# A gated mix of a long convolution and a mixer on one core: products as pairs of 128x64 tiles, and a new order of all tasks

## The chip, the cores and the metric

The kernel runs on one core of one Trainium2 chip. The metric is the device time of one execution in microseconds (us), the median of several runs; lower is better. A core has TensorE (PE: matrix products; its weight loads are listed apart as PEld), VectorE (DVE), ScalarE (ACT), GpSimd (POOL) and SyncE (SP), which here issues nearly all DMAs.

## The reference

`x` (2048 x 640, the input `q`) goes through two branches, and a gate mixes them.

```python
x = A_q
g = _sigmoid((x * gate_w).sum(-1, keepdims=True))
a = _A_ref(x, A_k, A_v, A_shift_k, A_ssm_k, A_ssm_D)
b = _B_ref(x, B_w1, B_w2, B_w3, B_w4)
return g * a + (1 - g) * b
```

Branch A: `k` is shifted and summed with four taps per channel and multiplied by `v` (that is `kv`); `kv` is convolved along the 2048 rows with a filter of 2048 taps per channel (the reference does it by an FFT of length 4096), `kv * ssm_D` is added, and the result is multiplied by `q`. Branch B, the mixer: layernorm, product with w1 (640x640), gelu, four groups of channels shifted by +1, -1, +2, -2 rows, product with w2, residual (`x1`); then layernorm, w3 (640x1536), gelu, w4 (1536x640), residual.

## The kernel before, in words

The whole kernel is a list of 778 **tasks**. Each has an engine (some have a choice), a duration that its author wrote down, what it reads and writes, and the buffers that it takes from pools and gives back. The text `ORDER` at the head of the file is a permutation of the task numbers; a letter behind a number names the engine where there is a choice. The function `place` walks the order, keeps a clock for each engine with the written durations, and picks buffers by it; then the tasks are issued in just this order. So the order of the text fixes the order on each engine. `place` also decides how many filler matmuls (L256, products of zeros that nobody reads) stand ahead of a PE task in the first microseconds, once the task `fill` has passed.

The convolution is a Fourier transform in steps, all of them matrix products on PE:

- `trh.0` to `trh.4` (L851) transpose the filter, loaded as `SK`; `evt.*` (L388 on ACT, L390 on DVE) copy the result to `HT`, and `dfold` (L857, POOL) adds the `ssm_D` row to it.
- `s1h.*` (L903) is the first step for the filter; it reads `HT` (the first four `evt` copies at least) and the matrix `BM`, which the DMA pair `bm` (L504) builds from the sine table. `s1x.*` (L905) is the same for `kv`. Their results are copied (`e1h`, `e1x`) to `FS` and written to memory (`wFh`, `wFx`, L935).
- `s2h`, `s2x` (L957) read them back (`rF`, L949) in ten parts; `pa`, `pb` (L972, DVE) multiply the spectra; `s3` (L985) goes back, `wG` writes.
- `s4.0` to `s4.15` (L1023) is the last step, one 128-row block each: two products of 512 columns and two of 128, each with a 128x64 weight tile, so that two run side by side in the two halves of the array. DVE then does `yq` (L1029, times the gate and q) and `ad` (L1056), or for the rows 12 to 15 `ax` (L1037) and `fo` (L1043), which add the mixer's part.

`kv` is made on DVE in four groups `kv3` to `kv0` of eight operations of 128x2560 each (L870, L874, L878): taps, sums and the product with `v`. The taps are the row `CJ`: `cjp` (POOL, L390) turns the order of 2560 numbers, `wCJ` (L516) writes them, `rCJ` (L518) reads them back on all partitions.

The mixer: `st1` (mean and variance of a block, DVE L578 to L582 or ACT L586, L587), `rs1` (POOL L595 to L598, the power -1/2), `nm1` (L602 or L632), `tr1` (L610, PE transposes, two blocks each), `ev1`, `evh` (copies to `xnT`), `w1.G.part` (L690, or L694 for part 4), `g1` (ACT L707, gelu), `w2.s` (L716), `x1.s` (DVE L723, residual), `sq.s` (ACT L728). The second half has `ve2`, `st2` (POOL), `nm2`, `dt2` (L805, a transposing DMA), `w3.c.fb` (L813, five products of 128x512), `g2` (ACT L820), `w4.s` (L827; L834 for the rows 12 to 15, as two tasks `.0` and `.1`): twelve products of 512 columns and twelve of 128. `t2.s` (DVE L842) adds it to x.

Each PE task has a **mode**, the shape of its weight tiles: `f` is 128x128, `c32` and `c64` are 128x32 and 128x64, `r64` 64x128, `q32` 64x32, `s32` 32x64. `place` adds 0.096 us where the mode of a PE task differs from that of the one before. In the kernel before, only `s4` has `c64`; `w3` and `w4` are all `f`.

PSUM is one pool of eight banks ("U"). A task takes one bank or an aligned pair, and the copy that reads it gives it back. At most eight DMAs of SP were under way at a time in the trace.

Of the kernel before, what the change touches and what calls it, by code (L numbers as in the profile page):

```python
# [37 lines left out]
41 0 23 5 29 94v 6 7 9 3 19 11 17 4 25 1 2 31 32 15 18 8 10 63v 12 13 14 26 27 87v 61a 85a 64 62 95v 104v 65v 28  # L38
42 88 86 393 24 44 96 209 43 210 55a 66v 89v 67 395 56 68a 58a 53v 54 97v 34 90a 30 399 396v 400v 57v 91 397 40
394a 93a 98 59 99v 100v 92v 60v 101 103v 143 147 16 20p 33 149 398a 102a 77a 145 79v 21 45 150 80 391 71v 72 46  # L40
22 144 148 69v 392v 82v 74a 121 39 122 450 70 78 146 107a 73v 458 35 75 451v 401p 438 37 81v 76v 439a 151 83
113v 123 36 459a 38 456 152 457a 49 84v 108 114 454 452 115v 116 125 455a 453a 110v 129 117v 446 444 126 460
118v 403 404 405 124 127 447a 162 163 406 130 128 156 157 440 105a 441a 407 159 153 154 106 160 461 47 445a 402
131 158 109a 155 442 111 132 137 443a 112a 408 161 462 466 48 138 409 463a 448 134 135 468 215p 216 449 164 140
469a 467a 119 413 141 51 221p 165 470 410 50 411 120a 166 222 223v 464 465a 167 474 471a 173 475a 174 171 217a
480 168 476 187 191 481a 482 193 477a 172 473 192 188 412 414 218 483a 478 169 195 189 170 181 415 416 417 479a
472 418 419 421 422 182 178 179 485 196 194 190 486 423 488 219a 484 225a 489a 175 220 487a 492 176 493a 136 203
424 204 494 425 490 206 498 207 495a 200 201 491a 420 426 427 428 430 502 499a 226 177 504 224 505a 211 503a 506
500 227 496 501a 239 507a 133 497 228 240 508 142 429 184 185 139 247 431 432 433 434 435 436 248 233 510 512
# [12 lines left out]
692v 691a 693 345 302 341 298 299 723 725 346 342 300 696 728 359 371 705 707 729 710 714 360 372 361 365 362
# [22 lines left out]
class Plan:  # L85
# [13 lines left out]
    def add(self, name, eng, dur, fn, r=(), w=(), use=(), acq=(), rel=(), roles=(), after=(), mode=None, nbytes=0):  # L99
# [3 lines left out]
        t.kept = None  # L103
        t.acq = [(a, 1, a == "U") if isinstance(a, str) else a for a in acq]
# [43 lines left out]
    def place(self, order):  # L148
# [6 lines left out]
        mode, bw, flying, self.kept = None, 0.0, [], None  # L155
        start, end = [None] * n, [None] * n
        for i in order:
# [34 lines left out]
            else:  # L192
                d = t.dur
# [17 lines left out]
                free[e] = end[i] = at + d  # L211
            for (o, p, k) in t.rel:
# [143 lines left out]
def build(env, nc, io):  # L356
# [55 lines left out]
    add("ident", "POOL", 0.55, c_id, r=["iotb"], w=["ID"])  # L412
# [100 lines left out]
    add("cjp", {"POOL": 3.2, "ACT": 2.3}, 0, lambda t: copy(t, env["VC"][0:1, 3, :, :],  # L513
# [106 lines left out]
    for s0 in pairs:  # L620
        nm = []
        for s in (s0, s0 + 1):
            st1[s] = add(f"st1.{s}", {"DVE": 1.26, "ACT": 1.73}, 0, lambda t, s=s: f_st1(t, s), r=[("x", s, 0), ("x", s, 1)],
                         w=[("MV", s)])
            add(f"rs1.{s}", "POOL", 0.85, lambda t, s=s: f_rs1(t, s), r=[("MV", s), "c0"], w=[("RS", s)])
        for s in (s0, s0 + 1):
# [7 lines left out]
            nm1[s] = add(f"nm1.{s}", {"DVE": 0.445, "ACT": 1.2}, 0, f_nm1, r=[("RS", s), ("x", s, 0), ("x", s, 1)],  # L634
# [154 lines left out]

    LATE, late = (12, 13, 14, 15), {}  # L790
    for c in range(4):
        nT, nP = None, f"x1nT{c % 2}"
        for s0 in (4 * c, 4 * c + 2):
            ss = (s0, s0 + 1)
            add(f"ve2.{s0}", {"DVE": 0.42, "POOL": 1.5}, 0, lambda t, s0=s0: f_ve2(t, s0), r=[("x", s, 0) for s in ss] + [("S2", s) for s in ss],
                w=[("v2", s0)])
            add(f"st2.{s0}", "POOL", 1.5, lambda t, s0=s0: f_st2(t, s0), r=[("v2", s0)] + [("x", s, 0) for s in ss],
# [12 lines left out]
        for fb in range(12):  # L810
            def w3(t, fb=fb, nP=nP):
                for kb in range(5):
                    nc.tensor.matmul(env.PS[:, t.buf["U"][0], :], lhsT=env["W3"][:, kb, 128 * fb:128 * fb + 128],  # L813
                                     rhs=env.nT(int(nP[-1]))[:, :, kb, :], start=(kb == 0), stop=(kb == 4))
            t = add(f"w3.{c}.{fb}", "PE", 1.09, w3, r=["W3"] + [("x1nT", 4 * c + i) for i in range(4)], rel=[(nT, nP)],
                    use=[h2] if h2 else [], acq=[ONE] if h2 else [ONE, "h2"], after=("xnT",), mode="f")
# [5 lines left out]
        for s in range(4 * c, 4 * c + 4):  # L822
            def w4(t, s=s, o=h2):
                m = env.Uf(t.buf["U"][0])
                for (c0, c1) in ((0, 512), (512, 640)):
                    for fb in range(12):
                        nc.tensor.matmul(m[:, c0:c1], lhsT=env["h2T"][:, o.buf["h2"][0], fb, 128 * (s % 4):128 * (s % 4) + 128],  # L827
                                         rhs=env["W4"][:, fb, c0:c1], start=(fb == 0), stop=(fb == 11))
# [270 lines left out]
```

## Time and profile before

| | us |
|---|---|
| median of 3 runs (lowest, highest) | 226.26 (226.03, 226.96) |
| span of the profiled execution, first to last instruction | 225.3 |
| what the median has beyond that span | 1.0 |
| PE busy | 214.4 (95%) |
| DVE busy | 188.8 (84%) |
| ACT busy | 154.7 (69%) |
| POOL busy | 45.9 (20%) |
| moved by DMA | 57.90 MB, mean 257 GB/s |

The profile is of one execution. For that execution there is its span alone, not a device time of its own; the median of the runs is 1.0 us above the span. A row of a timeline reads: start, length, engine, line, operation, output <- input with partitions x elements, count, and in brackets how long the engine was idle before and who ended it. A row of the chain reads: start, length, what, count. A matmul's own length covers its way through the array: 379 ns for 512 columns, though a stretch of 25 of them takes 5.50 us of the chain, 220 ns each; so a small gap between two matmuls does not show as idle PE, and PE's busy share says little of switches between tile shapes.

### The profile page before, as it was taken

The numbers are of one execution on the slowest core, as the hardware profiler recorded it, in microseconds if no ns is written. First come the engines' busy times: TensorE is split into PE (matmuls) and PEld (weight loads), VectorE is DVE, ScalarE is ACT, GpSimd is POOL, SyncE is SP. The second block draws the span as 40 slices with busy tenths as digits, with TensorE's granted clock in tenths as the row PEclk, the third lists the DMA queues.
The fourth block names the chain that finished last, engine by engine and source line by source line (L and its number), as shares of the span: only waits on it lengthen the run. The fifth ranks groups of instructions, "written<-read, shape, count | busy, mean of one in ns | idle before, by whom it ended". The sixth has DMA issues, their size and how long they took to land.

```text
span 225.3 us, 5017 instructions
## 1 busy us (share of the span) xinstructions
PE 214.4 (95%) x1978; PEld 104.2 (46%) x1998; DVE 188.8 (84%) x281; ACT 154.7 (69%) x225; POOL 45.9 (20%) x86
## 2 busy tenths in 40 slices
PE   3999999999999999999999999999999999999993
PEld 1576454556444444345543333334445554544462
DVE  7898897999999999997479989899767327988993
ACT  6988999699988999789568988878875002125000
POOL 7373451446100009920800000000000000000000
PEclk9999999999999999999999999999999999999998
DMA  6999998999999969979999969999982596888524
GB/s 194 274 335 244 238 245 255 292 225 355 322 210 368 205 231 298 378 254 246 237 390 311 305 190 288 279 323 340 221 269 87 160 414 188 256 268 249 166 58 116
DMA packets 39501, 57.90 MB, mean 257 GB/s; under 512 B 15027, under 2 KB 30645, under 8 KB 39478
## 3 DMA queue, kind: packets, MB, share of 16 engines
q1 hardware_dynamic: 39158, 57.27, 88.9%
q10 hardware_dynamic: 320, 0.33, 0.5%
q8 instruction: 15, 0.25, 0.4%
q14 instruction: 8, 0.07, 0.1%
HBM read 35.56 MB, written 18.36 MB: 239 GB/s over the span
## 4 chain that ended last, share of the span: by engine, by line
PE 72%; DVE 11%; DMA 9%; ACT 4%; issue 2%; POOL 1%; DVEq 0%; POOLq 0%
PE PS L813 18%; PE PS L827 17%; PE PS L716 9%; DMA C<-TRIG 7%; PE PS L834 6%; PE PS L957 5%; PE PS L690 4%; PE PS L985 4%; DVE VC L870 3%; DVE VC L874 3%; PE PS L1023 2%; DMA K<-in_A_k_dram 2%; ACT FS L388 2%; PE PS L256 2%; PE PS L903 2%
## 5 line engine op out<-in xcount | busy, mean ns | idle before, releaser
L820 ACT ACTIVATE h2T<-PS 128x512 bf16<-128x512 f32 x48 | 27.9, 605 | 28.4 <-PE PS L813 28.0
L827 PE MATMUL PS<-W,h2T 128*128 128x128 bf16 (+1 forms) x281 | 39.8, 297 | 0.4
L388 ACT CAST FS<-PS 128x1024 bf16<-128x1024 f32 x37 | 36.0, 1019 | 5.6 <-PE PS L905 3.5
L813 PEld LDWEIGHTS <-W 128*128 128x128 bf16 x240 | 21.1, 98 | 30.7 <-issue 9.4
L827 PEld LDWEIGHTS <-h2T 128*128 128x128 bf16 x288 | 22.2, 98 | 18.9 <-issue 1.9
L388 ACT CAST XH<-PS 128x1024 bf16<-128x1024 f32 x26 | 25.5, 1020 | 7.5 <-PE PS L957 7.4
L813 PE MATMUL PS<-x1nT,W 128*128 128x512 bf16 x120 | 28.5, 380 | 0.0
L813 PE MATMUL PS<-XB,W 128*128 128x512 bf16 x120 | 28.5, 380 | 0.0
L972 DVE TENSOR_TENSOR PP<-XH 128x2048 bf16<-128x2048 bf16 x20 | 23.7, 1220 | 3.1 <-ACT XH L388 2.8
L870 DVE TENSOR_TENSOR VC<-K,VC 128x2560 bf16<-128x2560 bf16 x16 | 23.7, 1491 | 1.7 <-DMA W<-in_B_w_dram 1.5
L716 PE MATMUL PS<-W,hsT 128*128 128x128 bf16 (+1 forms) x155 | 23.5, 297 | 1.0 <-ACT hsT L707 0.7
L842 DVE TENSOR_TENSOR x<-PS,x 128x640 bf16<-128x640 f32 x12 | 9.8, 824 | 13.7 <-PE PS L827 13.7
L690 PE MATMUL PS<-xnT,W 128*128 128x512 bf16 x80 | 19.2, 379 | 0.1
L716 PEld LDWEIGHTS <-hsT 128*128 128x128 bf16 x160 | 12.8, 98 | 13.1 <-DMA W<-in_B_w_dram 1.2
L874 DVE TENSOR_TENSOR VC<-VC 128x2560 bf16<-128x2560 bf16 x12 | 17.9, 1491 | 0.3
L390 DVE CAST XH<-PS 128x1024 bf16<-128x1024 f32 x14 | 16.9, 1220 | 1.2 <-PE PS L957 1.1
L1029 DVE SCALAR_TENSOR_TENSOR W<-PS,GG,QO 128x640 bf16<-128x640 f32 x16 | 13.6, 879 | 2.5 <-PE PS L1023 2.2
L388 ACT CAST GS<-PS 128x1024 bf16<-128x1024 f32 x12 | 12.0, 1016 | 3.9 <-PE PS L985 3.9
L256 PE MATMUL PS<-C 128*128 128x512 bf16 x34 | 10.7, 460 | 3.8 <-DVE C L507 3.7
L834 PE MATMUL PS<-W,h2T 128*128 128x128 bf16 (+1 forms) x94 | 13.3, 298 | 0.1
L723 DVE SCALAR_TENSOR_TENSOR x<-PS,x 128x640 bf16<-128x640 f32 x16 | 12.9, 820 | 0.3 <-PE PS L716 0.3
L957 PE MATMUL PS<-FX,TRIG 64*32 64x512 bf16 x320 | 12.4, 381 | 0.3 <-ACT GS L388 0.3
(115 smaller groups left out, 292.5 us busy)
## 6 DMA issues: line engine op xcount, KB each, us to landing
FH<-FS SPq DMA_DIRECT2D x8, 640.0 KB, 5.3
FXD<-FS SPq DMA_DIRECT2D x8, 640.0 KB, 5.4
FX<-FH SPq DMA_DIRECT2D x10, 512.0 KB, 5.8
FX<-FXD SPq DMA_DIRECT2D x10, 512.0 KB, 5.3
GX<-GD SPq DMA_DIRECT2D x8, 640.0 KB, 5.9
W<-in_B_w_dram SPq DMA_DIRECT2D x2, 1920.0 KB, 11.9
GD<-GS SPq DMA_DIRECT2D x8, 480.0 KB, 4.4
SK<-in_A_ssm_k_dram SPq DMA_DIRECT2D x5, 512.0 KB, 6.8
```

Source lines behind the costliest of these rows:

```text
L388: nc.scalar.copy(out=out, in_=in_)
L390: (nc.vector if t.on == "DVE" else nc.gpsimd).tensor_copy(out=out, in_=in_)
L690: nc.tensor.matmul(m[:, b, :], lhsT=W[:, 0, kb, 160 * fb:160 * fb + 128], rhs=rhs(kb, shifts[fb]), start=(kb == 0), stop=(kb == 4))
L716: nc.tensor.matmul(m[:, c0:c1], lhsT=env["hsT"][:, o.buf["hs"][0], fb, 128 * (s % 4):128 * (s % 4) + 128], rhs=env["W12"][:, 1, fb, c0:c1] ...
L813: nc.tensor.matmul(env.PS[:, t.buf["U"][0], :], lhsT=env["W3"][:, kb, 128 * fb:128 * fb + 128], rhs=env.nT(int(nP[-1]))[:, :, kb, :], star ...
L820: nc.scalar.activation(out=env["h2T"][:, o.buf["h2"][0], fb, :], in_=env.PS[:, t.buf["U"][0], :], func=ACT.Gelu_apprx_tanh)
L827: nc.tensor.matmul(m[:, c0:c1], lhsT=env["h2T"][:, o.buf["h2"][0], fb, 128 * (s % 4):128 * (s % 4) + 128], rhs=env["W4"][:, fb, c0:c1], st ...
L834: nc.tensor.matmul(env.PS[:, t.buf["U"][0], 0:c1 - c0], lhsT=env["h2T"][:, o.buf["h2"][0], fb, 128 * (s % 4):128 * (s % 4) + 128], rhs=env ...
L870: nc.vector.tensor_tensor(out=VC[:, o], in0=env["K"][:, a + 3 - j:a + 7 - j, :], in1=w, op=ALU.mult)
L874: nc.vector.tensor_tensor(out=VC[:, 1], in0=VC[:, 1], in1=VC[:, 2], op=ALU.add)
L957: nc.tensor.matmul(env.U(t.buf["U"][0])[32 * j:32 * j + 32, gp, :], lhsT=CRI()[64 * gp:64 * gp + 64, 32 * pc:32 * pc + 32], rhs=X[64 * gp: ...
L972: nc.vector.tensor_tensor(out=env["PP"][:, o.buf["PP"][0], a, :].rearrange("p (b c) -> p b c", b=2), in0=X.unsqueeze(1).broadcast_to([P, 2 ...
```

## The change

Three things are changed.

- **Tiles.** The function `halves_of` gives, for a task of mode `c64`, the two halves of 64 columns. With it, every product of `w3.3.*` (12 tasks), of `w4.8`, `w4.10`, `w4.11`, and of `w4.12` to `w4.15` is issued as two products with 128x64 weight tiles, side by side like those of `s4`, and these tasks have mode `c64`. That makes 228 products into 456 (144 of them had 512 columns, 84 had 128).
- **Durations in `place`.** Those of several GpSimd tasks (`ident`, `cjp`, `rs1`, `ve2`, `st2`, `dfold`) and of `st1` and `nm1` are other numbers, and DVE tasks of some kinds are not placed while `cjp` or `dfold` runs on GpSimd. This acts on the choice of buffers and on the count of fillers only.
- **Order.** `ORDER` is another permutation, with other engine letters.

```diff
 ORDER = """
-41 0 23 5 29 94v 6 7 9 3 19 11 17 4 25 1 2 31 32 15 18 8 10 63v 12 13 14 26 27 87v 61a 85a 64 62 95v 104v 65v 28
...
+23 5 6 0 7 1 9 3 11 12 104v 8 10 17 2 15 29 63v 64 94v 61a 32 25 28 97v 95a 55v 62 65v 66v 96 19 31 87v 67 98 53a 54 ...
...
+    LOCKS = ("nm1.", "nm2.", "kv", "pa.", "pb.", "pc.", "ad.", "ax.", "phase1", "phand", "phsmall")
...
+            t.lock, t.hold = t.name.startswith(self.LOCKS), t.name in ("cjp", "dfold")
...
+                if t.lock and e == "DVE" and held[0] <= at < held[1]:
+                    start[i] = at = held[1]
...
-    add("cjp", {"POOL": 3.2, "ACT": 2.3}, 0, lambda t: copy(t, env["VC"][0:1, 3, :, :],
+    add("cjp", {"POOL": 2.6, "ACT": 2.3}, 0, lambda t: copy(t, env["VC"][0:1, 3, :, :],
...
+    def halves_of(t):
+        return ((0, 64), (64, 64)) if t.mode == "c64" else ((0, P),)
+
     LATE, late = (12, 13, 14, 15), {}
+    COLS = (8, 10, 11, 12, 13, 14, 15)
...
-                    nc.tensor.matmul(env.PS[:, t.buf["U"][0], :], lhsT=env["W3"][:, kb, 128 * fb:128 * fb + 128],
-                                     rhs=env.nT(int(nP[-1]))[:, :, kb, :], start=(kb == 0), stop=(kb == 4))
+                    for q, w in halves_of(t):
+                        nc.tensor.matmul(env.PS[q:q + w, t.buf["U"][0], :], lhsT=env["W3"][:, kb, 128 * fb + q:128 * fb + q + w],
+                                         rhs=env.nT(int(nP[-1]))[:, :, kb, :], start=(kb == 0), stop=(kb == 4))
...
-                    use=[h2] if h2 else [], acq=[ONE] if h2 else [ONE, "h2"], after=("xnT",), mode="f")
+                    use=[h2] if h2 else [], acq=[ONE] if h2 else [ONE, "h2"], after=("xnT",), mode="c64" if c == 3 else "f")
...
-                        nc.tensor.matmul(m[:, c0:c1], lhsT=env["h2T"][:, o.buf["h2"][0], fb, 128 * (s % 4):128 * (s % 4) + 128],
-                                         rhs=env["W4"][:, fb, c0:c1], start=(fb == 0), stop=(fb == 11))
-            kw = dict(r=["W4"] + [("h2", c, fb) for fb in range(12)], rel=[(h2, "h2")], mode="f")
+                        for q, w in halves_of(t):
+                            a = 128 * (s % 4) + q
+                            nc.tensor.matmul(m[q:q + w, c0:c1], lhsT=env["h2T"][:, o.buf["h2"][0], fb, a:a + w],
+                                             rhs=env["W4"][:, fb, c0:c1], start=(fb == 0), stop=(fb == 11))
+            kw = dict(r=["W4"] + [("h2", c, fb) for fb in range(12)], rel=[(h2, "h2")], mode="c64" if s in COLS else "f")
```

The new order in the places that matter, by task names.

- SP, head, before: ldsk1 ldx4 ldCJ ldgw ldx0 ldx14 ldx2 ldsk2 ldD ldsk4 ldsk3 ldw1 ldx6 ldsk0 bm ldx10 wCJ ldk15 ldk11 rCJ. After: ldx4 ldx14 ldgw ldx2 ldCJ ldx0 ldx6 ldsk4 ldw1 ldx10 ldsk3 ldsk2 ldsk0 ldD ldsk1 wCJ bm ldk11 ldk15 rCJ. (`ldx` loads blocks of x, `ldsk` the filter, `ldk` k.)
- ACT, head, after: warm abs sin0 st1.4 st1.14 st1.2 st1.0 st1.8 sin1 sin st1.7 st1.9 ev1.14 g1.1.2 st1.6 g1.0.0 st1.11 g1.0.2 g1.0.4 g1.0.1 g1.0.3 nm1.6 evt.0 nm1.10 e1h.4. Before, six `st1` were on ACT and ten on DVE; after, nine and seven. evt.0 was on DVE and is on ACT.
- PE, head, after: tr1.4 tr1.14 tr1.2 tr1.0 fill gwm w1.1.2 w1.0.3 w1.0.0 w1.0.4 w1.0.2 trh.3 w1.0.1 trh.2 trh.0 tr1.8 trh.1 tr1.6 trh.4 s1h.4 s1h.5 w1.1.1 w1.1.3 s1h.6 w1.1.0 s1h.7 tr1.10. Before, `fill` came first, and 36 filler matmuls were issued; after, one.
- DVE, ahead of the kv groups, after: ... evt.4 st1.13 e1h.6 ev1.10 kv3.m2. From kv3 to kv0.v both orders hold 32 kv operations and 15 x1; before also nm2.2, after also sg.
- PE, last stage, before: w4.9 w4.6 | s4.6 s4.7 w3.3.0 w3.3.6 s4.2 s4.3 w3.3.1 ... , seven stretches of s4 among products of mode f. After: w4.7 w4.9 | w3.3.0 w3.3.4 w3.3.11 w3.3.10 s4.6 s4.7 w3.3.2 s4.3 s4.2 ... w4.12.1, all of one mode behind the bar; w4.10 and w4.11 stand behind the bar as well.
- Places where the mode of a PE task differs from the one before it: 97 before, 84 after. Of these, with c64: 14 before, 1 after; with q32 or s32 (the steps s2 and s3): 51 before, 57 after; with r64 or c32: 32 before, 26 after.

More of the change, by code (lines that the diff above doesn't have):

```diff
@@ L211, in place @@
                 free[e] = end[i] = at + d
+                if t.hold and e == "POOL":
+                    held = (at, end[i])
             for (o, p, k) in t.rel:
@@ L622, in build @@
         for s in (s0, s0 + 1):
-            st1[s] = add(f"st1.{s}", {"DVE": 1.26, "ACT": 1.73}, 0, lambda t, s=s: f_st1(t, s), r=[("x", s, 0), ("x", s, 1)],
+            st1[s] = add(f"st1.{s}", {"DVE": 1.37, "ACT": 1.7}, 0, lambda t, s=s: f_st1(t, s), r=[("x", s, 0), ("x", s, 1)],
                          w=[("MV", s)])
-            add(f"rs1.{s}", "POOL", 0.85, lambda t, s=s: f_rs1(t, s), r=[("MV", s), "c0"], w=[("RS", s)])
+            add(f"rs1.{s}", "POOL", 0.95, lambda t, s=s: f_rs1(t, s), r=[("MV", s), "c0"], w=[("RS", s)])
         for s in (s0, s0 + 1):
@@ L633, in f_nm1 @@
                                             scalar2=SS("RS")[:, c], op0=ALU.add, op1=ALU.mult)
-            nm1[s] = add(f"nm1.{s}", {"DVE": 0.445, "ACT": 1.2}, 0, f_nm1, r=[("RS", s), ("x", s, 0), ("x", s, 1)],
+            nm1[s] = add(f"nm1.{s}", {"DVE": 0.445, "ACT": 0.95}, 0, f_nm1, r=[("RS", s), ("x", s, 0), ("x", s, 1)],
                          acq=("xn",))
@@ L794, in build @@
             ss = (s0, s0 + 1)
[L795 removed]
+            add(f"ve2.{s0}", {"DVE": 0.42, "POOL": 4.0}, 0, lambda t, s0=s0: f_ve2(t, s0), r=[("x", s, 0) for s in ss] + [("S2", s) for s in ss],
                 w=[("v2", s0)])
[L797 removed]
+            add(f"st2.{s0}", "POOL", 3.5, lambda t, s0=s0: f_st2(t, s0), r=[("v2", s0)] + [("x", s, 0) for s in ss],
                 w=[("r2", s) for s in ss])
@@ L856, in build @@
         add(f"evt.{cb}", {"ACT": 1.86, "DVE": 1.23}, 0, evt, use=[t], rel=[(t, "U")], w=[("HT", cb)], after=("PRE",), roles=("HT",))
-    add("dfold", {"DVE": 0.5, "POOL": 0.9}, 0, lambda t: (nc.vector if t.on == "DVE" else nc.gpsimd).tensor_tensor(out=env["HT"][0:1, 0, :], in0=env["HT"][0:1, 0, :],
+    add("dfold", {"DVE": 0.5, "POOL": 1.5}, 0, lambda t: (nc.vector if t.on == "DVE" else nc.gpsimd).tensor_tensor(out=env["HT"][0:1, 0, :], in0=env["HT"][0:1, 0, :],
                                                                in1=env.early("DR", [1, D], BF16), op=ALU.add),
```

37 lines of the change are left out of this document (9 added, 28 removed), and 4 rows, old and new, of the table ORDER.

## The prediction

> **What bounds the kernel now.** I read the page's busy shares and chain first, then the windows of the stages, then the chain of the last stage.
>
> ```profile
> span 225.3 us, 5017 instructions
> PE 214.4 (95%) x1978; PEld 104.2 (46%) x1998; DVE 188.8 (84%) x281; ACT 154.7 (69%) x225; POOL 45.9 (20%) x86
> PE 72%; DVE 11%; DMA 9%; ACT 4%; issue 2%; POOL 1%; DVEq 0%; POOLq 0%
> ```
>
> PE is the bound on average. An average over stages says little, so the next view cuts the span at five events: first operation of the kv groups (37.33), end of the last one (96.97), first product of s2 (113.59), first product of s4 (186.30), end of PE (221.50).
>
> ```profile
> core 0: us, PE busy (x) PEld busy (x) DVE busy (x) ACT busy (x) POOL busy (x), PEclk, DMA share, GB/s
> 0.00:37.33 37.33, 32.35 (x277) 18.73 (x282) 31.53 (x96) 32.92 (x49) 18.99 (x44) 1.00 0.95 257
> 37.33:96.97 59.64, 58.65 (x421) 28.27 (x424) 58.31 (x64) 53.18 (x81) 21.84 (x27) 1.00 0.99 282
> 96.97:113.59 16.62, 16.34 (x123) 8.86 (x123) 10.58 (x26) 12.05 (x23) 5.10 (x16) 1.00 0.98 264
> 113.59:186.30 72.71, 72.02 (x927) 31.22 (x932) 56.40 (x55) 49.62 (x62) 0.00 (x0) 1.00 0.92 273
> 186.30:221.50 35.20, 35.04 (x242) 17.08 (x244) 31.51 (x41) 6.94 (x12) 0.00 (x0) 1.00 0.67 194
> 221.50:225.30 3.80, 0.02 (x1) 0.00 (x0) 0.41 (x2) 0.00 (x0) 0.00 (x0) 0.78 0.40 109
> ```
>
> The reader is to see that the stages have different limits. In the first, ACT (32.9 of 37.3) and DVE (31.5) are as full as PE, and part of PE's time is fillers:
>
> ```profile
> L256 PE MATMUL PS<-C 128*128 128x512 bf16 x34 | 10.7, 460 | 3.8 <-DVE C L507 3.7
> ```
>
> In the second, DVE is busy for 58.31 of 59.64 us: the kv groups are one chain on one engine, so what comes behind them (the last s1x, the write and read through memory, s2) moves with the **start of kv3**. From s2 on PE is busy 99% and decides; there the number of switches between tile shapes counts. What a switch costs is in the chain of the last stage.
>
> ```profile
> 186.34 0.66 PE PS L1023 x8
> 187.00 2.27 PE PS L813 x10
> 192.19 0.94 PE PS L1023 x12
> 199.59 5.50 PE PS L813 x25
> ```
>
> L813 is w3: 25 products take 5.50 and 10 take 2.27, so one costs (5.50-2.27)/15 = 0.215 us, and 2.27-10x0.215 = 0.12 is left over for the switch. L1023 is s4: four more products cost 0.94-0.66 = 0.28 us, and 0.66-0.56 = 0.10 is left. So **a switch costs 0.11 us** in either direction.
>
> **The change part by part. Tiles.** In the last stage 14 switches become 1: 13x0.11 = -1.43 us. In s2 and s3 the new order has 57 instead of 51: +0.66. The other six saved lie ahead of the end of kv, where DVE decides; they count nothing. Together **-0.77**.
>
> What the pairs themselves cost: an s4 block is one pair of 512 and one of 128 columns, 0.28 us. The same work with full tiles in w4 is 0.215 plus a 128-column product. Of these twelve in a row have to be loaded at their own pace:
>
> ```profile
> L834 PE MATMUL PS<-W,h2T 128*128 128x128 bf16 x48 | 3.2, 219 | 0.0
> L834 PEld LDWEIGHTS <-h2T 128*128 128x128 bf16 x96 | 7.3, 98 | 5.9 <-issue 0.5
> L1023 PEld LDWEIGHTS <-BT 128*64 128x64 bf16 x64 | 2.5, 109 | 3.6 <-issue 2.5
> ```
>
> In an unbroken stretch one of them costs about 0.06 us (the busy row's 3.2/48 = 0.067 still holds the tail of each dozen), so a pair of 512 and one of 128 should cost 0.275 with full tiles: the s4 block's 0.28 is the same within what can be read. The unknown is a dozen small pairs in a row, which s4 never has. Below: no loss, as in s4 (a gain is excluded: the columns streamed are as many). Above: the load of a half tile is 109-98 = 11 ns longer; if all of it shows, 84 pairs x 0.011 = +0.9. I take 0, because in s4 the loads behind a small pair had no more than that pair's 0.06 us either; both ends stay in the range.
>
> **Order, head.** Today kv3 waits for a DMA at its start, and the first product of s1h stands at 28.23:
>
> ```profile
> 28.23 0.38 PE L903 MATMUL PS<-HT,C 128*128 128x512 bf16 x1 [0.58 <-DVE HT L390]
> 37.33 1.49 DVE L870 TENSOR_TENSOR VC<-K,VC 128x2560 bf16<-128x2560 bf16 x1 [1.51 <-DMA W<-in_B_w_dram]
> ```
>
> The bytes that SP issues ahead of the taps (x, filter, w1, bm, eight blocks of k) are the same in both orders, so kv3 can hardly start ahead of 37.3. What the new order puts ahead of it is ACT: s1h.4 needs evt.0, and evt.0 now stands on ACT behind nine st1.
>
> ```profile
> 3.49 1.15 ACT L486 ACTIVATE PRE<-PRE,C 128x1024 f32<-128x1024 int32 x1 [1.28 <-DVE PRE L472]
> 4.67 2.56 ACT L484 ACTIVATE TRIG<-PRE,C 128x1024 bf16<-128x1024 f32 x3
> 7.14 0.72 ACT L586 ACTIVATE JK<-x 128x640 bf16<-128x640 bf16 x1
> 8.94 0.74 ACT L586 ACTIVATE JK<-x 128x640 bf16<-128x640 bf16 x1
> L388 ACT COPY xnT<-PS 128x1280 bf16<-128x1280 bf16 x4 | 4.9, 1227 | 1.9 <-DVE xnT L390 1.0 <-PE PS L610 0.9
> L707 ACT ACT_TABLE_LOAD x1 | 1.3, 1283 | 0.0
> L707 ACT ACTIVATE hsT<-PS 128x512 bf16<-128x512 f32 x20 | 11.3, 611 | 1.1 <-PE PS L690 1.0
> L602 ACT ACTIVATE xn<-x,NB,RS 128x640 bf16<-128x640 bf16 x4 | 3.6, 918 | 0.0
> L388 ACT COPY HT<-PS 128x2048 bf16<-128x2048 bf16 x2 | 3.7, 1858 | 0.0
> ```
>
> One st1 on ACT is 8.94-7.14 = 1.80. From 3.49 (DVE's phases, which release it, keep their place): abs 1.15, sines 2.56, nine st1 16.2, ev1.14 1.23, table 1.28, six g1 3.67, nm1.6 0.92, evt.0 1.86: 28.9, so evt.0 ends at **32.4**. ACT should not wait in between: x is now loaded first, and 40 transposes and the six w1 parts stand on PE ahead of where ACT needs them. Behind it PE has, up to tr1.10, by these rows:
>
> ```profile
> 42.70 0.43 PE PS L903 x2
> 53.57 0.56 PE PS L610 x10
> 54.13 1.08 PE PS L690 x5
> L390 DVE COPY xnT<-PS 128x1280 bf16<-128x1280 bf16 x4 | 3.2, 816 | 0.0
> ```
>
> four s1h 1.72, three w1 parts 3.24, tr1.10 0.56: 5.5, to 37.9 (38.2 with 0.3 for handing over banks); then ev1.10 on DVE, 0.82, and kv3 starts at about **39.1, +1.8**. Bounds: 37.3 (all of it hidden) and 41 (fillers, below). From there to the end of kv0 DVE has the same 32+15 operations, less nm2.2 plus sg:
>
> ```profile
> L604 DVE TENSOR_SCALAR xn<-x,r,SB 128x640 bf16<-128x640 bf16 x10 | 4.3, 439 | 0.4 <-POOL SB L788 0.4
> 100.45 13.21 PE L827 MATMUL PS<-W,h2T 128*128 128x512 bf16 x95
> ```
>
> That is -0.44, and sg, a sum of five numbers, under 0.2: **-0.3**. So the end of kv0 moves by +1.5, and s2 with it: the four w4 that cover the way through memory (13.2 us of PE in the second row) stand behind the last s1x in both orders. One s1x copy, e1xr.0, now stands on DVE behind two nm2 more; if the cover gets too short by that, up to 1 us more.
>
> **Order, behind.** PE idles for 0.69 us between 113.6 and 186.3: so much can be won at most. DVE gets three copies more there, 3.7 us, in 72.7 us with 56.4 busy; that fits. In the last stage w4.10 and w4.11 now stand behind the first s4, so DVE has two t2 more:
>
> ```profile
> L390 DVE CAST XH<-PS 128x1024 bf16<-128x1024 f32 x14 | 16.9, 1220 | 1.2 <-PE PS L957 1.1
> L842 DVE TENSOR_TENSOR x<-PS,x 128x640 bf16<-128x640 f32 x12 | 9.8, 824 | 13.7 <-PE PS L827 13.7
> ```
>
> 31.5+1.6 = 33.1 in a stretch of about 36.0 (35.2, plus two w4 of 3.3 and less the four w3 of 1.08 now ahead of the first s4, less 1.4 of switches). It fits with little to spare; up to +1 where one late input puts DVE last. I take 0 for both. The GpSimd durations change no instruction. The tail (3.80 us) keeps its form: an `fo` of 128 columns, one store.
>
> **Sum** against the profiled execution: 225.3 + 1.5 - 0.8 + 0 = 226.0 of span. The median is 1.0 above the span of the profile, so **227.0**, that is +0.7 on 226.26.
>
> **The rivals.**
>
> 1. *Slower: PE comes cold to w1.* Fillers now run while PE waits:
>
> ```profile
> 3.72 4.88 PE L256 MATMUL PS<-C 128*128 128x512 bf16 x11 [3.72 <-DVE C L507]
> L851 PE MATMUL PS<-ID,SK 128*128 128x128 bf16 x80 | 5.8, 226 | 0.4 <-DVE HT L390 0.3
> ```
>
> The first eleven cost 0.44 each, twice the later 0.215, while the granted clock reads 1.00. The new order has one filler, so the first products at the slow rate are w1's own. PE's work between w1 (about 17, an estimate: four st1 on ACT end at 13.0, then rs1, nm1, tr1 and ev1) and s1h.4 (32.4) is six w1 parts, five trh, two tr1: 6.5+5.8+1.1 = 13.4 of 15.4 us, 2 us to spare. Each slow product takes 0.22 more, so from nine on they delay kv3; all thirty would be 6.6 - 2.0 = +4.6. With some twenty slow ones, +2.4: **229.4**. For: nothing but transposes runs ahead of w1. Against: from 17 on PE is nearly dense. (The Trainium skill, "TensorE: Matmul & The Clock Gate", Part 1, has the slow rate end after about 3.4 us of sustained activity; by that eight products would be slow, no delay. The first eleven fillers, 4.88 us, say a little more.) Also here: SP stands at wCJ until cjp, now behind rs1.9, is done; bm, k and the taps queue behind it.
>
> 2. *Faster: kv3 starts at 37.3 as before.* If copies and PE run ahead of my ACT sum, the taps' DMA decides again. Then -0.3 - 0.8, and with the 0.69 us of idle PE won, -1.8: **224.5 to 225.2**. For: x comes first, so PE can begin w1 earlier. Against: the ACT sum.
>
> 3. *The half loads come one after the other.* Then a small pair costs two loads, 2x0.109 = 0.218 at worst and, overlapping as the full ones do, about 0.11 instead of 0.06: 84x0.05 = +4.2: **231.2**. Against: s4's 0.28. (The Trainium skill, "TensorEngine Tiling (Array Packing)", Restrictions, says that column tiling switches Fast Weight Load off, which speaks for this rival; s4 does not show it.)
>
> 4. *The change saves no switch:* the 0.11 us belongs to s4's own start, not to the change of shape. Then the sum lacks 1.4: **228.4**.
>
> **How the numbers follow.** Forecast 0.44 (its own range 226.2 to 228.0: same 0.30, slower 0.14); rival 1 0.22 (slower); rival 2 0.24 (faster 0.20, same 0.04); rival 3 0.05 and rival 4 0.05 (slower). So faster by over 0.5% 0.20, same 0.34, slower 0.46; 0.5%, 1.1 us, is about what a measurement of this kernel can tell from no change. The range reaches from rival 2's middle to rival 1's place: 224.8 to 229.6; left out are the far end of rival 1, rival 3 and the best of rival 2.
>
> **What would show it.** Head: evt.0 (L388 to HT on ACT) ending near 32.4, the first L870 near 39.1 with no DMA as releaser. kv0.v ending near 98.5, s2 starting near 115. Last stage: L1023 and L813 without the 0.11 left over, some 1.4 us shorter for the same work; L834's small pairs at 0.06. Wrong if L870 starts at 37.3 (rival 2) or after 40 (rival 1: look for L690 products 0.43 apart), if the small pairs take 0.1, or if PE has new idle time in s2 and s3 or DVE ends last by more than the final `fo`.

## The result, and the profile after

The changed kernel takes **229.98 us** (median of 5 runs, 229.72 to 230.40) against 226.96 for the kernel before in the same session (226.26 in the table above). One of the five executions of before in that session, 231.02 us, was in a slower state of the chip and is left out of the ratio; the other four have a median of 226.6. The ratio is **1.015, with a 95% interval of 1.012 to 1.018**: slower by 3.4 us, where +0.7 was forecast. The profiled execution took 230.4 us; its span is 228.6.

The page of the changed kernel, three lines that answer to those shown of before:

```profile
span 228.6 us, 5415 instructions
PE 208.2 (91%) x2177; PEld 105.3 (46%) x2191; DVE 190.6 (83%) x269; ACT 154.2 (67%) x232; POOL 50.2 (22%) x92
PE 58%; DVE 14%; ACT 9%; DMA 8%; SPq 6%; issue 4%; POOL 0%; DVEq 0%; POOLq 0%; ACTq 0%
```

PE is busy for 6 us less (before, the fillers alone took 10.7 us of it), and its share of the chain falls from 72% to 58%: DVE, ACT and SP's queue (SPq) have moved into the chain, the DMAs themselves have not (9% before, 8% now). The windows, cut at the corresponding events (start of kv3, end of kv0.v, first product of s2, first product of the last stage, end of PE), say where the time went. The last stage begins here with w3.3.0, since four w3 now stand ahead of the first s4.

```profile
0.00:40.01 40.01, 27.04 (x234) 17.40 (x236) 30.73 (x85) 34.35 (x60) 20.37 (x50) 1.00 0.88 251
40.01:99.30 59.29, 57.36 (x430) 28.23 (x435) 58.05 (x65) 52.90 (x79) 25.66 (x30) 1.00 0.95 270
99.30:116.53 17.23, 16.95 (x121) 8.69 (x122) 10.82 (x26) 10.68 (x22) 3.34 (x10) 1.00 1.09 266
116.53:184.61 68.08, 66.61 (x878) 27.35 (x884) 57.33 (x53) 49.35 (x62) 0.80 (x3) 1.00 0.88 256
184.61:224.89 40.28, 40.24 (x521) 23.68 (x520) 33.35 (x43) 6.95 (x12) 0.00 (x0) 1.00 0.76 238
```

Two w4 of about 3.27 us each (twelve products of 512 and twelve of 128; 3.26 without a switch in a chain shown below) have changed sides, from the fourth stage to the fifth; with 6.54 us moved, before's stages are 66.17 and 41.74.

| | before | after | difference | forecast |
|---|---|---|---|---|
| start of kv3 | 37.33 | 40.01 | +2.68 | +1.8 |
| kv3 to end of kv0.v | 59.64 | 59.29 | -0.35 | -0.3 |
| kv0.v to s2 | 16.62 | 17.23 | +0.61 | 0 |
| s2 to last stage, same work | 66.17 | 68.08 | +1.91 | +0.66 |
| last stage, same work | 41.74 | 40.28 | -1.46 | -1.43 |
| end of PE | 221.50 | 224.89 | +3.39 | +0.7 |

The tiles' share came out as forecast. The loss has two main places, the head and the middle. Of the 2.7 us by which the forecast missed, 1.25 are in the middle, 0.88 at the start of kv3 and 0.61 ahead of s2. In the head, this is what DVE, ACT and PE did (timelines of the changed kernel):

```profile
19.56 1.20 ACT L369 COPY xnT<-PS 128x1280 bf16<-128x1280 bf16 x1
20.80 2.43 DVE L371 COPY xnT<-PS 128x640 bf16<-128x640 bf16 x5 [5.23 <-ACT xnT L369]
16.91 4.13 PE L671 MATMUL PS<-xnT,W 128*128 128x512 bf16 x10 [0.21 <-DMA W<-in_B_w_dram]
22.47 1.24 PE L671 MATMUL PS<-xnT,W 128*128 128x512 bf16 x5 [1.43 <-DVE xnT L371]
28.20 1.08 ACT L688 ACTIVATE hsT<-PS 128x512 bf16<-128x512 f32 x2 [0.73 <-PE PS L671]
30.47 1.87 ACT L369 COPY HT<-PS 128x2048 bf16<-128x2048 bf16 x1 [0.38 <-PE PS L841]
32.11 1.23 DVE L371 COPY HT<-PS 128x2048 bf16<-128x2048 bf16 x1 [0.18 <-PE PS L841]
33.48 1.02 PE L893 MATMUL PS<-HT,C 128*128 128x512 bf16 x3
39.27 0.82 DVE L371 COPY xnT<-PS 128x1280 bf16<-128x1280 bf16 x1 [0.86 <-PE PS L591]
40.01 2.88 DVE L860 TENSOR_TENSOR VC<-K,VC 128x2560 bf16<-128x2560 bf16 x2
```

Read it from the second row. DVE stands idle for **5.23 us** until ACT's copy in the first row (`ev1.14`, the main copy of tr1.14) has ended; then it does `evh.14`, the halo copies of the same transposes. PE's third part of w1 (w1.0.0, fourth row) waits for that halo, and all that follows on PE is late by it: the transposes of the filter, the copy of evt.1 on DVE (seventh row, ending at 33.34), and so s1h, which needs it. evt.0 on ACT, which the forecast took for the last input of s1h, ended at 32.34, as forecast; it was not the last. The first ten products of w1 ran at the slow rate (4.13 us, against 2.15 at 0.215 each), which is rival 1's picture, but PE then waited 1.43 us for DVE all the same.

### The profile page after: what moved, and what is told of

The parts are those of the page before. It is cut to its first block, busy times and chain, and to the rows that moved or that the text cites. A ratio compares the mean times of both kernels' runs of the same rounds, so it can differ in the third digit from the quotient of the medians.

```text
span 228.6 us, 5415 instructions
## 1 busy us (share of the span) xinstructions
PE 208.2 (91%) x2177; PEld 105.3 (46%) x2191; DVE 190.6 (83%) x269; ACT 154.2 (67%) x232; POOL 50.2 (22%) x92
## 4 chain that ended last, share of the span: by engine, by line
PE 58%; DVE 14%; ACT 9%; DMA 8%; SPq 6%; issue 4%; POOL 0%; DVEq 0%; POOLq 0%; ACTq 0%
PE PS L799 21%; PE PS L815 11%; PE PS L824 6%; PE PS L947 4%; PE PS L975 4%; PE PS L697 4%; DMA FX<-FH 4%; DVE VC L860 3%; ACT FS L369 3%; DVE VC L864 3%; DMA FX<-FXD 2%; SPq L790 2%; SPq L364 2%; PE PS L1013 2%; ACT JK L709 2%
## 5 line engine op out<-in xcount | busy, mean ns | idle before, releaser
L815 PE MATMUL PS<-W,h2T 128*128 128x128 bf16 (+3 forms) x354 | 40.2, 298 | 0.3
L799 PEld LDWEIGHTS <-W 128*128 128x128 bf16 (+1 forms) x300 | 22.0, 102 | 30.4 <-issue 9.5
L815 PEld LDWEIGHTS <-h2T 128*128 128x128 bf16 (+1 forms) x360 | 22.9, 103 | 17.9 <-issue 1.1
L799 PE MATMUL PS<-XB,W 128*64 128x512 bf16 (+1 forms) x180 | 28.8, 380 | 0.0
L369 ACT CAST XH<-PS 128x1024 bf16<-128x1024 f32 x21 | 20.9, 1017 | 10.7 <-PE PS L947 10.6
L371 DVE CAST XH<-PS 128x1024 bf16<-128x1024 f32 x19 | 23.2, 1220 | 3.4 <-PE PS L947 3.3
L671 PE MATMUL PS<-xnT,W 128*128 128x512 bf16 x80 | 21.2, 406 | 1.6 <-DVE xnT L371 1.4
L591 PE MATMUL PS<-ID,xn 128*128 128x128 bf16 x80 | 7.9, 265 | 11.1 <-DVE xn L613 11.1
L824 PE MATMUL PS<-W,h2T 128*64 128x512 bf16 (+1 forms) x192 | 13.5, 299 | 0.0
L671 PEld LDWEIGHTS <-W 128*128 128x128 bf16 x80 | 7.7, 103 | 12.2 <-issue 5.0
```

The lines of the kernel that those rows point to most:

```text
L369: nc.scalar.copy(out=out, in_=in_)
L371: (nc.vector if t.on == "DVE" else nc.gpsimd).tensor_copy(out=out, in_=in_)
L671: nc.tensor.matmul(m[:, b, :], lhsT=W[:, 0, kb, 160 * fb:160 * fb + 128], rhs=rhs(kb, shifts[fb]), start=(kb == 0), stop=(kb == 4))
L799: nc.tensor.matmul(env.PS[q:q + w, t.buf["U"][0], :], lhsT=env["W3"][:, kb, 128 * fb + q:128 * fb + q + w], rhs=env.nT(int(nP[-1]))[:, :, ...
L815: nc.tensor.matmul(m[q:q + w, c0:c1], lhsT=env["h2T"][:, o.buf["h2"][0], fb, a:a + w], rhs=env["W4"][:, fb, c0:c1], start=(fb == 0), stop= ...
L824: nc.tensor.matmul(env.PS[q:q + w, t.buf["U"][0], 0:c1 - c0], lhsT=env["h2T"][:, o.buf["h2"][0], fb, a:a + w], rhs=env["W4"][:, fb, c0:c1] ...
```

## Experiments

Theory H: the head is late because evh.14 stands on DVE behind ev1.14 on ACT. Theory Q: the middle is late because of SP's new order of transfers. Rivals: the pairs cost something; the cold TensorE (rival 1 of the prediction); ACT's sum of work (the prediction's own step); the changed rest as a whole. Medians are given with the ratio to the kernel before on the same chip and its 95% interval, and differences are taken between ratios, times 226.7.

**The two parts alone.** `tiles_only` is the order of before, with pairs; w4.10 and w4.11 stay full there, since they stand among full products.

```diff
-    COLS = (8, 10, 11, 12, 13, 14, 15)
+    COLS = (8, 12, 13, 14, 15)
 ORDER, and the written durations: those of the kernel before
```

> The kernel before with its own order; only the tile pairs are put in: the 12 products of w3 of chunk 3, w4.8 and w4.12 to w4.15 run as pairs of 128x64. Theory A (the order is what made the change slower, the pairs do what they say): the 13 switches between full tiles and the last step of the convolution go at 0.11 us each, so 1.4 us less than before, about 225.0. Theory B (the pairs cost something, half rate or weight loads that show): 0 to 4 us more than before.

Measured: 225.46 us, ratio **0.996 (0.993 to 0.999)**. `order_only` is the changed order with

```diff
-        return ((0, 64), (64, 64)) if t.mode == "c64" else ((0, P),)
+        return ((0, P),)
```

> The changed kernel's order with full 128x128 tiles everywhere, as before. Theory A: the switches that the pairs save in this order come back, 10 groups of the last step stand among the mixer's products, 19 switches more at 0.11 us, so 2.1 us more than the changed kernel, about 232. Theory B (pairs cost): no more than the changed kernel, or less, 226 to 230.

Measured: 231.54 us, ratio 1.021 (1.017 to 1.025). So the order alone costs 4.7 us and the pairs win: 0.9 us in the old order (13 switches), 1.3 us in the new one (19 switches). By the traces it is more: the last stage of `order_only` takes 42.55 us against 40.28, that is 2.27, where 19 switches at 0.11 are 2.1. The chain of `order_only` there, and then that of the changed kernel:

```profile
189.46 1.19 PE PS L799 x5
190.64 0.66 PE PS L1013 x8
191.31 2.27 PE PS L799 x10
208.69 3.37 PE PS L815 x24
```

```profile
189.05 0.54 PE PS L1013 x8
189.59 1.08 PE PS L799 x10
191.22 2.16 PE PS L799 x20
207.46 3.26 PE PS L815 x48
```

Every stretch is 0.11 to 0.12 us shorter with pairs (1.19 to 1.08, 0.66 to 0.54, 2.27 to 2.16, 3.37 to 3.26), and in each row twice the products are at no greater price. (The Trainium skill, "TensorEngine Tiling (Array Packing)", Restrictions, says that column tiling switches Fast Weight Load off. No cost of it shows here: 48 half products take 3.26 us, 24 full ones 3.37 with their switch, which is 3.26 without.) In `tiles_only` the stage takes 33.98 us instead of 35.20, 1.22 less and not 1.43; its chain runs over DVE alone from 209.9 on, so there DVE has become the last to finish.

**Head and rest crossed.** `oldhead` has everything up to the first s2 in the old order and the rest in the new one, `oldrest` the reverse, both with pairs.

```diff
 oldhead:  ORDER = (before, up to task 535) + (after, without those)
 oldrest:  ORDER = (after, up to task 535) + (before, without those)
```

> Tile pairs in; everything up to the first product of the convolution's second step (s2) in the order and on the engines of the kernel before, the rest in the changed order. Theory A1 (the head is the main loss: kv3 2.7 us late): s2 starts at about 113.6 as before; the rest then costs what it costs in the changed kernel, 1.9 more in the middle and 1.5 less at the end: about 0.4 us more than before, 226.9. Theory A2 (the waits of the middle come from the late head as well): 0.66 more of switches and 1.4 less: about 225.7. Theory A3 (the rest is the main loss): 229 or more.

> Tile pairs in; the changed order up to the first product of s2, the rest in the order of the kernel before (w4.10 and w4.11 full there). Theory A1: s2 starts 2.9 us late as in the changed kernel and the rest is as before without 13 switches: 2.9 less 1.4, about 227.9. Theory A3 (the head's delay is taken up later, the rest is the loss): 225 to 226.

Measured: `oldhead` 229.79 (1.012, 1.008 to 1.015), `oldrest` 229.57 (1.011, 1.008 to 1.014). Each half alone seemed to cost nearly what both cost together. But `oldhead` had a wait that neither kernel has:

```profile
117.04 0.14 PEld L947 LDWEIGHTS <-TRIG 64*32 64x32 bf16 x16 [2.71 <-DMA FX<-FXD]
```

The splice had put dt2.8, a transposing DMA that waits for nm2.8, on SP's queue ahead of the first read of the k side, and s2 stood for the read. Two repairs:

```diff
 oldhead:  ... 305v 306 258 347v 348 535 ... 547v 550 ...        (305 nm2.8, 306 dt2.8, 550 rFh.1)
 oldhead2: ... 258 347v 348 535 ... 547v 305v 306 550 ...
 oldhead3: ... 305v 258 347v 348 535 ... 547v 306 550 ...
```

> As oldhead, but the transpose of nm2.8 (and nm2.8) stands behind the first five reads of s2's blocks; in oldhead it stood ahead of the first read of the k side, and TensorE waited 2.71 us for that read. Theory A1 (the changed middle costs 0.66 of switches and about 1 of waits, the pairs give 1.4): 226.5 to 227.2. Theory A3 (the changed rest is a main loss whatever the head): 228.5 or more.

`oldhead2` was a mistake: 236.72 us (1.045, 1.041 to 1.048). nm2.8 itself had come late, and SP stood for it with every later read behind:

```profile
109.84 1.11 SPq L939 DMA_DIRECT2D FX<-FXD  x2
125.27 1.21 SPq L790 DMA_TRANSPOSE x1nT<-xn  x1
130.69 0.15 PEld L947 LDWEIGHTS <-TRIG 64*32 64x32 bf16 x16 [7.42 <-DMA FX<-FH]
```

SP did nothing from 110.95 to 125.27, and PE waited 7.42 us at its next block. (The rows are of SP's and PE's timelines.) It tells nothing of A1 or A3, only what one late input costs on a queue that is worked in order.

> As oldhead (the head of the kernel before, the rest in the changed order, pairs in), but only the transfer of nm2.8's transpose is moved behind the first five reads of s2's blocks; nm2.8 itself stays where it was. oldhead2 moved nm2.8 as well, and SP stood 14 us for it. Theory A1 (the changed middle costs 0.66 of switches and about 1 of waits, the pairs give 1.4): 226.5 to 227.2. Theory A3 (the changed rest is a main loss whatever the head): 228.5 or more.

`oldhead3`: **226.29 us, 0.998 (0.996 to 1.001)**, a little under A1's range. The crossing:

| ratio to before, all with pairs | old rest | new rest |
|---|---|---|
| old head | 0.996 | 0.998 |
| new head | 1.011 | 1.015 |

The new head costs 1.5% to 1.7% (3.4 to 3.8 us), the new rest 0.2% to 0.4% (0.5 to 0.9). So the head is the main loss, and A3 fell. Between A1 and A2 (the waits of the middle come with the late head) the medians can't decide, but the trace speaks against the 1 us of waits that A1 took for granted: the changed rest behind the old head takes 66.63 us from s2 to the last stage, not 68.08.

```profile
113.25:179.88 66.63, 66.63 (x882) 27.17 (x880) 57.53 (x55) 49.35 (x62) 3.25 (x6) 1.00 0.91 262
```

**What in the head.** `evh_first` exchanges two neighbours in the text of the order; `evh_warm` also puts the zeros and the filler products first, as before; `warm_only` does that alone.

```diff
-... 79a 102a 103v 92v ...      (102 ev1.14 on ACT, 103 evh.14 on DVE)
+... 79a 103v 102a 92v ...      (evh_first, evh_warm)
-23 5 6 0 ...
+23 5 17 18 6 0 ...             (17 zeros, 18 fill; evh_warm, warm_only)
```

> The changed kernel with one pair of tasks exchanged: evh.14 (DVE, the halo copies of tr1.14) ahead of ev1.14 (ACT, the main copy) in the order. Theory H (the head is late because DVE stands 5.23 us for ACT's copy, and w1.0.0 behind it): w1.0.0 starts at 21.0 instead of 22.47, ACT's gelus and evt.0 come 1.1 earlier, kv3 starts at 38.9 instead of 40.01, and the kernel is 1.1 us shorter, about 228.9. Rival (ACT's sum of work alone sets evt.0 and kv3): kv3 stays within 0.3 of 40.0, no gain.

> As evh_first, and TensorE is kept busy from the start as in the kernel before: the zeros and the filler products stand first, 26 fillers ahead of tr1.4 and 14 more up to tr1.0. Rival 1 of the prediction (the cold TensorE is what costs): the first ten products of w1 take 2.2 us instead of 4.13, and kv3 and the end come 1 to 2 us earlier than in evh_first. Theory H (ACT's queue is full from 19.6 on and sets the gelus): the ten products take 2.2 us, but kv3 starts as in evh_first within 0.3, and the time is the same.

> The changed kernel with TensorE kept busy from the start (zeros and filler products first), and nothing else: evh.14 stays behind ev1.14. Rival 1 of the prediction (the cold TensorE is what makes the changed kernel slow): about 2 us less than the changed kernel, 228. Theory H (DVE's wait for ACT's copy ends at 20.8 whatever TensorE's rate, and w1.0.0 starts at 22.5 behind it): w1.0.0 starts at 22.5, kv3 within 0.5 of 40, no gain, 229.5 to 230.5.

Measured: `evh_first` **227.83 (1.005, 1.003 to 1.008)**, `evh_warm` **227.44 (1.002, 0.999 to 1.005)**, `warm_only` **230.35 (1.017, 1.012 to 1.022)**. The exchange wins 2.2 us, the warm TensorE with it perhaps 0.7 more (the intervals overlap), and by itself nothing. In the trace of `evh_warm` kv3 starts at 37.59, as in `evh_first`, so nothing of the 0.7 is in the head there. The head of `evh_first`:

```profile
14.74 3.15 DVE L371 COPY xnT<-PS 128x1280 bf16<-128x1280 bf16 x6
18.04 3.41 PE L671 MATMUL PS<-xnT,W 128*128 128x512 bf16 x15 [1.45 <-DMA W<-in_B_w_dram]
29.12 1.88 ACT L369 COPY HT<-PS 128x2048 bf16<-128x2048 bf16 x1
29.57 1.23 DVE L371 COPY HT<-PS 128x2048 bf16<-128x2048 bf16 x1 [0.17 <-PE PS L841]
31.05 1.02 PE L893 MATMUL PS<-HT,C 128*128 128x512 bf16 x3
37.58 2.88 DVE L860 TENSOR_TENSOR VC<-K,VC 128x2560 bf16<-128x2560 bf16 x2
```

The halo copies are done in one go (x6 instead of x5 after a gap), w1.0.0 follows w1.0.3 without a gap, and kv3 starts at **37.58**, 2.43 earlier and 0.25 from where it was before. My expectation was 1.1: I had counted the 1.43 of waiting, and not that in this execution the products ran at the full rate, so that w1.0.0 could start at 20.2 (18.04 + 10 x 0.215) and not at 21.04. evt.0 ends at 31.00, with ACT waiting for nobody from 3.49 on. And `warm_only`:

```profile
17.62 2.33 PE L671 MATMUL PS<-xnT,W 128*128 128x512 bf16 x10 [1.32 <-DMA W<-in_B_w_dram]
20.80 2.43 DVE L371 COPY xnT<-PS 128x640 bf16<-128x640 bf16 x5 [5.10 <-ACT xnT L369]
22.48 2.26 PE L671 MATMUL PS<-xnT,W 128*128 128x512 bf16 x5 [2.53 <-DVE xnT L371]
```

The first ten products are fast now, and PE just waits longer, 2.53 instead of 1.43, for the same halo at 22.48. (kv3 then starts at 41.38, outside the 0.5 that I had allowed: the clock dipped while w1.0.0 ran, see the last section.) `order_only` shows the same without a filler; its instructions in the head are those of the changed kernel, and its first ten products happened to be fast:

```profile
17.19 2.33 PE L671 MATMUL PS<-xnT,W 128*128 128x512 bf16 x10 [0.49 <-DMA W<-in_B_w_dram]
22.47 1.37 PE L671 MATMUL PS<-xnT,W 128*128 128x512 bf16 x5 [2.95 <-DVE xnT L371]
```

In all five traces with evh.14 behind ev1.14, w1.0.0 starts between 22.46 and 23.11 and kv3 between 39.99 and 41.38, whether the ten products took 2.33 us or 4.13. With evh.14 first, kv3 starts at 37.58, 37.59 and 37.60, and at 39.46 in `mended`, where the clock dipped. So the slow rate is not what made the changed kernel slow. No trace has evh.14 first and slow products; what the exchange wins then is not shown.

Why does DVE wait for ACT? In the built program the first copy of evh.14 has a wait on ACT's semaphore, and with the two tasks exchanged it has none (listing of DVE's instruction 51, changed kernel and `evh_first`):

```
51 L371 TensorCopy xnT<-PS 128x10x64 [waits Activation_49]
51 L371 TensorCopy xnT<-PS 128x10x64
```

The two copies read the same pair of PSUM banks. In a variant that was only built, in which evh.14 reads another pair, the wait is not there. So the framework puts two readers of one bank on different engines one after the other, in the order of the text. (The Trainium skill, "PSUM — Partial Sum Buffer", PSUM bank collisions raise a hardware error, gives the reason: two engines must not access the same bank and quadrant at once, reads against reads included, and the compiler's scheduler adds a dependency for it. The wait in the trace agrees; no run here shows a collision.) The plan does not know of it: evh.14 and ev1.14 write different keys (`("xnT", -2)` and `("xnT", 14)`) and have only tr1.14 in common. Worked out with its written durations, `place` starts evh.14 at 16.0 and ev1.14 at 18.4, side by side with other work; an order searched with this model can't see the 5.23 us.

**What in the middle.** Of the 1.91 us, the six more switches should be 0.66. The rest are waits of PE for the reads of s2's blocks. The chain of the changed kernel at the longest of them, a row of SP's queue ahead of it, and PE's weight load behind it:

```profile
149.06 0.61 PE PS L947 x16
...
150.13 8.05 DMA FX<-FH
...
158.22 0.63 PE PS L947 x16
```

```profile
141.42 6.54 SPq L996 DMA_TRANSPOSE BT<-XB  x1
```

```profile
158.22 0.14 PEld L947 LDWEIGHTS <-TRIG 64*32 64x32 bf16 x16 [1.49 <-DMA FX<-FH]
```

The read of one block was issued at 150.13 and landed 8.05 us later (the page has 5.9 as the median of these reads), behind the transpose BT<-XB, at which SP's queue was busy for 6.54 us. The load of such a block stands 0.42 us anyway (the rows of `order_only` below), so the wait costs 1.07, and one more at 118.60, of 0.76, costs 0.34. `dbt_late` moves that transpose:

```diff
-... 320 695 608 ... 678 673 ...      (695 dbt, 678 rFh.9)
+... 320 608 ... 678 695 673 ...
```

> The changed kernel with one transfer moved: the transpose BT<-XB (dbt) stands behind the last read of s2's blocks instead of ahead of five of them. Theory Q (the reads behind dbt land late, 8 us for one of them, and TensorE waits 1.49 us): that wait goes, s3 ends 1 to 1.5 us earlier, the kernel is about 229. Rival (the waits only move on to the next transfer, or the last stage waits for BT): no gain, or up to 1 us more.

Measured: 229.36 us, 1.013 (1.009 to 1.016). In the trace, the stage from s2 on:

```profile
116.67:183.61 66.94, 66.46 (x876) 27.28 (x880) 57.16 (x53) 49.35 (x62) 0.52 (x3) 1.00 0.89 259
```

That is 1.14 less than 68.08, as theory Q said. By the medians the win is 0.6 us, which the intervals don't separate from nothing. And theory Q is not shown: runs that have the transpose in its early place, ahead of the same read, show anything from a longer wait to none. `evh_first`, then `order_only` with its load of the same block and its stage:

```profile
155.33 0.14 PEld L947 LDWEIGHTS <-TRIG 64*32 64x32 bf16 x16 [2.07 <-DMA FX<-FH]
```

```profile
158.08 0.16 PEld L947 LDWEIGHTS <-TRIG 64*32 64x32 bf16 x16 [0.42 <-issue]
```

```profile
117.79:184.31 66.52, 66.31 (x876) 27.30 (x881) 56.64 (x52) 49.33 (x62) 0.05 (x1) 1.00 0.88 259
```

`evh_warm` stands 0.95 us there (stage 67.14), `warm_only` 0.51 and `oldhead3` 0.42 (66.63); the two runs with the transpose moved, `dbt_late` and `mended`, stand 0.42. So the early transpose alone does not make the wait; whether it makes it more likely, one trace of each order can't say. Where there is no wait, the stage is 0.35 to 0.46 us longer than before's 66.17: the six switches, a little under the 0.66. With everything together,

> The changed kernel with its two stalls taken out: evh.14 ahead of ev1.14 with TensorE warm (evh_warm) and BT<-XB behind the last read of s2's blocks (dbt_late). If the two add: 2.5 and 0.6 to 1.1 less than the changed kernel, 226.2 to 226.9. Theory of the sum: what is left against the kernel before is 0.66 of switches in the middle and 1.4 less at the end, about 226. Rival (the middle waits for something else when the head is earlier, as in oldhead): no gain over evh_warm, 227.4.

`mended` takes **226.58 us, 1.001 (0.998 to 1.003)**. The changed order with both repairs and with pairs is as fast as the order before without pairs. Whether the two repairs add can't be told: by the ratios `mended` is 0.3 us faster than `evh_warm`, within the intervals, so the rival (no gain over `evh_warm`) is not excluded. Last, the mended head with the old rest:

```diff
 newhead_best: ORDER = (evh_warm, up to task 535) + (before, without those); COLS as in tiles_only
```

> Tile pairs in; the changed order up to s2 with evh.14 ahead of ev1.14 and TensorE warm, the rest in the order of the kernel before. It is oldrest without the head's stall. Theory of the sum: oldrest's 229.57 less the 2.5 that evh_warm won against the changed kernel gives 227.0. Theory H in full (the stall is the whole of the head's loss, and oldrest's later end of DVE came from it too): as tiles_only, 225.0 to 225.8.

Measured: 226.58 us, 0.997 (0.993 to 1.001), on a chip where the kernel before took 227.35. Against `oldrest` that is 3.1 us less by the ratios. As ratios the two expectations are 1.000 (the sum) and 0.992 to 0.996 (theory H in full): the measured 0.997 lies nearer to the second, and its interval holds both. `tiles_only` (0.996) remains the version that beats both kernels with some certainty; `newhead_best` can't be told from it.

## Why the prediction was wrong

Two steps failed: the head was reckoned without a wait that decided it, and the middle was put at nothing but its switches. Part by part:

- **The tiles: right.** 1.43 forecast in the last stage, 1.46 measured; a switch at 0.11; the dozen small pairs at no price, the lower bound. Rivals 3 and 4 fell with `order_only` and `tiles_only`.
- **The head: the failed step.** The prediction put it as "ACT should not wait in between: x is now loaded first, and 40 transposes and the six w1 parts stand on PE ahead of where ACT needs them", and priced the head by ACT's sum alone: evt.0 at 32.4, kv3 at 39.1 (+1.8; measured +2.68). evt.0 did end at 32.34, but by luck, by two errors that cancel: without any wait it ends at 31.00 (`evh_first`), so the sum was 1.4 too long (0.8 of it the six g1, 0.61 each in the sum and 0.48 from start to start), and ACT waited 0.73 and 0.38 for PE, which stood behind DVE, which stood behind ACT's ev1.14. What failed is "ACT should not wait" and that evt.0 comes last: s1h needed evt.1 too, and that came at 33.34 because DVE had stood 5.23 us. Behind s1h the reckoning was right (6.7 us to kv3 forecast, 6.53 measured; its own terms add up to 39.0, not 39.1). The step looked for who needs ACT's results by data and left out who shares a PSUM bank with it. Yet the profile of before had the row, quoted in the prediction: `L388 ... 1.9 <-DVE xnT L390 1.0`, ACT standing for DVE's halo copies, the same pair in the other order:

```profile
22.11 1.23 ACT L388 COPY xnT<-PS 128x1280 bf16<-128x1280 bf16 x1 [1.04 <-DVE xnT L390]
```

Read as a dependency, it would have shown that the new order makes DVE wait until ACT is through with the seven st1 that stand ahead of ev1.14. Without the stall s1h does start right behind evt.0 (31.05), on the path that the prediction took, and kv3 starts at 37.58: near rival 2's 37.3, but not released by a DMA, as rival 2 had it. So the forecast of +1.8 came from a sum that was 1.4 too long, and the +2.68 from a wait that it left out. Nor is 37.3 the floor that the prediction took it for: with the old head kv3 started between 36.26 (`oldhead`) and 37.53 (`tiles_only`).
- **kv0.v to s2:** 0 taken, +0.61 measured, inside the +1 kept as a bound. It belongs to the new head: the nine traces with it take 16.81 to 17.98 us there, the five with the old head 16.61 or 16.62. Its cause was not tried.
- **The middle: mis-sized.** "PE idles for 0.69 us ... so much can be won at most ... I take 0 for both" looked at what the new order could win and at DVE's load, not at what it could lose on SP's queue. The term was +0.66 and measured +1.91, in the profiled execution. What it left out are waits for the reads of s2's blocks, 1.4 us of them; why they come in some runs and not in others (`order_only`, `oldhead3`) stays open.
- **Rival 1** was right in sign and near in time (229.4), but not by its mechanism: the ten slow products were there (4.13 us), and `warm_only` took them away for nothing. (The Trainium skill, "TensorE: Matmul & The Clock Gate", Part 1, has the slow rate end after some 3.4 us and calls the moment run-variable. That it varies agrees: with the same instructions on PE the first ten products took 4.13 us in the changed kernel, 3.88 in `dbt_late`, 3.74 in `oldrest` and 2.33 in `order_only`. The 3.4 us can't be read off here: in the changed kernel all ten were slow, where the prediction reckoned eight by it.)

The sum that the runs give: 2.4 for the stall, 0.6 on the way to s2, 0.5 for the switches in the middle and 1.4 for the waits there (together the 1.91), less 1.5 for the tiles: +3.4. Only the first and the last of these were shown by an experiment; what is left at kv3 (+0.25) and the kv groups (-0.35) nearly cancel.

## What to carry to other kernels

Two engines that read one PSUM bank are one queue: whichever stands first in the program goes first, however long it has to wait for its own turn, so put the reader first whose engine is free. A planner that does not know this will place both copies side by side. A change that keeps its promise (1.4 us here, by the trace) can be lost in an order that was searched anew along with it, so measure the two apart first. And before a wait for a DMA is put down to the transfer ahead of it, look whether other runs with that transfer in the same place have the wait.

## What the runs showed of the hardware that was not expected

- **The rate of TensorE's first products is not set by fillers alone.** `evh_first` did nothing until 16.6 but transposes at the slow rate (1.25 us for ten, 0.72 later), five products of one column and one filler, and its first 15 products of w1 ran at the full rate (3.41 us); the changed kernel, with the same instructions on PE up to there, ran ten in 4.13 us. The granted clock reads 1.00 in both.
- **A dip of the granted clock.** `warm_only` had the granted clock at 0.51 from 23 to 26 us, just when w1.0.0 ran (2.26 us for five products); `mended` had one at 20 to 23 and took 5.10 us for the first 15 products, where `evh_warm`, with the same instructions, took 3.41. In those two profiled executions kv3 starts 1.4 us later than in the changed kernel and 1.9 later than in `evh_warm`. `order_only` had one too (0.57 from 23 to 26), and kv3 1.3 us later than the changed kernel. What sets it off was not tried.

```profile
23.00:26.00 3.00, 3.00 (x21) 0.84 (x22) 2.79 (x9) 2.54 (x7) 1.04 (x3) 0.51 0.86 252
```

```profile
18.34 5.10 PE L671 MATMUL PS<-xnT,W 128*128 128x512 bf16 x15 [2.05 <-DMA W<-in_B_w_dram]
```

```profile
18.14 3.41 PE L671 MATMUL PS<-xnT,W 128*128 128x512 bf16 x15 [1.85 <-DMA W<-in_B_w_dram]
```
